# A planned attention and two-layer kernel: the planner's costs, the group sizes of two blocks, and the place of one block's sums

## The chip, the cores and the metric

The kernel runs on one core of a Trainium2 chip. The metric is the device time of one execution in microseconds (us). The engines are TensorE (PE, with its weight loads PEld), VectorE (DVE), ScalarE (ACT), GpSimd (POOL) and SyncE (SP, which here only issues transfers). Each engine works off its own queue of instructions in order and waits on semaphores for the others.

## The reference

Eight batches, eight heads, 576 positions, head width 64. First a masked, decaying attention without softmax, then a two-layer network over the 4608 tokens that it yields:

```
scores = (1/sqrt(D)) * q @ k.T
Dmat   = where(rel >= 0, gamma[h] ** rel, 0)      # rel = i - j
x      = (scores * Dmat) @ v                      # to (tokens, heads*64)
h      = x @ w_in                                 # 512 -> 2048
out    = (h * cos(h)) @ w_out                     # 2048 -> 512
```

Inputs and output are float32. The kernel multiplies in bfloat16 and adds up in float32.

## The kernel before, in words

**Attention.** The work is cut into units `(b, g)`: batch `b`, and `g` = 0, 1 for 256 positions each, 2 for the last 64. A unit's q, k and v come in by three loads of 512 KB on SP (`stgq`, `stgk`, `stgv`, line 471). k is cast (`natk`, line 462), q and v are scaled by the decay (`qnat`, `natv`, line 504), mostly on POOL; the first two units are marked fast and use DVE and ACT too. k and q are then transposed: for blocks 0 and 1 by PE (line 525) with a copy out of PSUM by ACT or DVE, from block 2 on by SP's transposing transfers (`kt`, `qt`, line 540). PE makes the scores (`bk<-qt,kt`), DVE multiplies them by the triangular mask (four operations of 512 columns to a unit, `pt`, line 611), and PE makes the outputs (`bk<-pt,natv`, with `qt` times the running state, all on line 571). The state `st` is built by PE from k and v and copied out by ACT (`sba`, `sbb`, `sbr`). Two copies on ACT (line 461) bring a unit's outputs to `xt`. Two units, those of two neighbouring batches, fill one block of 512 tokens: block 0 is (0,0) and (1,0), block 1 (0,1) and (1,1), block 2 (2,0) and (3,0), block 3 (2,1) and (3,1), and so on; block 8 is made of the eight short units.

**First layer** (`mlp1`, lines 762 to 773). For each of 16 slices `f` of the hidden width, PE runs four matmuls into one of six PSUM banks (`bk<-xt,win`), ACT makes the sine (`cb`, line 770; a shift of pi/2 makes it a cosine), and DVE multiplies the two into `gt` (line 773). `ses` says which units of the block a group covers: one of them (256 tokens, a half group) or both (512, a full group). The order of the slices is `FORDER`: 0 to 3, 8 to 11, 4 to 7, 12 to 15, four for each of the four slabs of `win`, which arrive in the order 0, 2, 1, 3. Before, blocks 0, 1 and 2 are made by half groups: block 0 by a loop of its own in `graph`, which takes all halves of the first unit and then all of the second; blocks 1 and 2 by `SPLIT = 2`. Blocks 3 to 8 are made by full groups.

**Second layer** (`wino2`, lines 810 to 891). Each block needs 7 products P1 to P7 instead of 8, as in Strassen's and Winograd's scheme: halves of `gt` and quarters of `wout` are added and subtracted first. DVE makes eight sums for a block (S1 to S4, each in two parts of 1024 columns, `s`, lines 828 and 834), and once, for all blocks, eight differences of the weights (`wsums`, `tw` and `wout`, line 807). Each product is two pieces of eight matmuls (line 867: `bk<-wout,gt` for P1 and P2, `bk<-tw,s` for P6 and P5, `bk<-wout,s` for P7 and P3, `bk<-tw,gt` for P4). ACT copies three results aside (`sn`), DVE adds (`os`, line 879), and SP stores the two halves of a block.

**Weights.** `win` and `wout` come in by four loads each, issued by POOL (lines 742 and 746) and cast on the way. Loads on SP and POOL are gated on each other by hand (`gate`): the third unit's loads on `win` 2, `wout` on q of unit (1,1), and unit (2,0)'s loads on `wout` 2.

**The order of the work** is not written out by hand. `graph` makes a list of tasks, each with an engine, an estimated length, what it reads and writes, the buffers that it takes, and a priority, a due time derived from `T0`, `T1` and `PERIOD`. `Graph.run` then plays all of this through once, on the host, while the kernel is built: it puts each engine's tasks in the order in which they would start by the estimates, and hands out the buffers. The estimates are plain numbers in the code: `dma` and `tail` are a transfer's time on the shared DMA engines and from its end to its landing, and `port=True` keeps a DVE task and a POOL task from being planned at the same time. What comes out is one fixed queue for each engine. The estimates have no other effect: on the chip each instruction starts when its queue and its semaphores let it. A PE task that takes more than two PSUM banks can claim them when it is due (`due` in `pick`), so that smaller tasks do not take them one by one. Where the plan shows PE idle early on, the emitter puts in matmuls on a tile of ones (`warm`, line 409).

Of the kernel before, what the change touches and what calls it, by code (L numbers as in the profile page):

```python
# [11 lines left out]
B, H, S, D = 8, 8, 576, 64  # L12
# [117 lines left out]
class Graph:  # L130
# [3 lines left out]
    AHEAD, FETCH = 2000, 6500  # L134

# [72 lines left out]
    def run(self, dma_rate):  # L208
        self.prios()
        free = {e: 0.0 for e in ("pe", "act", "dve", "pool", "sp")}  # L210
# [3 lines left out]
        est, order = {}, []  # L214
# [19 lines left out]
        def pick(e):  # L234
            cand = []
            for t in ready[e]:
# [3 lines left out]
                s = max(free[e], est[t], a)  # L240
# [9 lines left out]
            if e == "pe":  # L250
                due = [t for t in ready[e] if all(any(f is not None and f <= free[e] + 1500 for f in self.pools[b.pool])
                                                  for b in t.allocs if b.pool != "bk") and self.first(t) and sum(b.pool == "bk" for b in t.allocs) > 2 and est[t] <= free[e] + 1500]
# [70 lines left out]
class Kernel:  # L323
# [7 lines left out]
    SPLIT = 2  # L331
# [127 lines left out]
    def copy(self, eng, dur, dst, src, r, w, **kw):  # L459
        if eng == "act":  # L460
            return self.one(eng, dur, lambda e: e.activation(dst(), src(), AF.Copy), r=r, w=w, **kw)  # L461
        return self.one(eng, dur, lambda e: e.tensor_copy(dst(), src()), r=r, w=w, port=True, **kw)  # L462


    def load(self, which, u, rows, gate):

        stg = self.staged[which, u] = Buf("stg" + which)
        src = self.src["qkv".index(which)]
        for i, (p0, n, o, ny, b, r0) in enumerate(rows):
            at, w = (b * H * S + r0) * D, ny * D  # L470
            self.one("sp", 500, lambda e, p0=p0, n=n, o=o, w=w, at=at: e.dma_start(  # L471
                ap(self.at(stg), 1024, p0, n, o, [w, H], [1, w]), bass.AP(src, at, [[w, n], [S * D, H], [1, w]])),
                r=gate, w=[(stg, i)], sem=lambda i=i: f"{which}{stg.slot}_{i}", dma=1830 if ny == 2 else 600, tail=720)
        return stg

    def unit(self, u, fast=False, gate=()):
# [3 lines left out]
        for which, nat, dst in (("k", "natk", "kt"), ("q", "qnat", "qt"), ("v", "natv", None)):  # L480
# [4 lines left out]
            stg = self.load(which, u, rows, gate)  # L485
            rs = [(stg, i) for i in range(len(rows))]
            nb = t[nat] = Buf(nat)
            for y in range(2):
# [8 lines left out]
                if which == "k":  # L497
                    eng = ("act", "pool")[y] if fast else "pool"
                    self.copy(eng, {"act": 520, "dve": 610, "pool": 560}[eng], out, inp, rs, [(nb, y)])
                else:  # L500
# [3 lines left out]
                    self.one(eng, 610 if eng == "dve" else 1000, lambda e, out=out, inp=inp, tab=tab, col=col, hs=hs: e.tensor_tensor(  # L504
                        out(), inp(), ap(tab, 40, 0, 128, col, *hs, [0, D]), ALU.mult),
                        r=rs + [(key,)], w=[(nb, y)], port=True)
# [29 lines left out]
    def txb(self, u):  # L536
        parts = []
# [6 lines left out]
        self.G.add("sp", 2600, parts, dma=4300)  # L544
# [104 lines left out]
    def outputs(self, u, prio, late, join=None):  # L649
# [57 lines left out]
        def copies():  # L707
            for s in range(2):
# [6 lines left out]
                self.copy("act", 590, dst, src, [(ob[s],)], [(xt, half, s)])  # L715
# [24 lines left out]
    def load_w(self, which, s, gate, prio):  # L740
# [4 lines left out]
        else:  # L745
# [4 lines left out]
                 sem=f"{which}{s}", dma=2600, tail=1500, prio=prio)  # L750
# [59 lines left out]
    def wino2(self, j, base, span):  # L810

        gt = self.gt[j]
        S_ = {(i, q): Buf("s") for i in range(1, 5) for q in range(2)}

# [9 lines left out]
        for q in range(2):  # L824
            for i, x, y, r, op in (
# [3 lines left out]
                         r=r, w=[(S_[i, q],)], port=True, name=f"S{i}_{j}")  # L829
        for q in range(2):  # L830
            for i, x, y, r, op in (
# [3 lines left out]
                         r=r, w=[(S_[i, q],)], port=True, name=f"S{i}_{j}")  # L835
# [71 lines left out]
    def graph(self):  # L907
# [103 lines left out]
```

## Time and profile before

| | us |
|---|---|
| median of 3 runs (302.33 to 304.1) | 303.77 |
| the profiled execution | 302.27 |
| its span, first to last instruction | 300.6 |
| PE busy (x3785 matmuls) | 284.7 |
| VectorE busy | 224.1 |
| ScalarE busy | 169.2 |
| GpSimd busy | 104.2 |
| mean granted TensorE clock | 0.999 |

The profile is one execution. A row of a timeline is: start, length, engine, line, operation, what it writes and reads, shape, count; in brackets the idle time of the engine ahead of it and what ended that. A row of a group ends with busy time, mean ns of one, and idle time ahead of them with what ended it. Lengths of neighbouring instructions overlap a little, since the engines are pipelined, so the time from start to start is shorter than the length. "L867" is line 867 of the kernel before; the kernel after has four lines more.

### The profile page before, as it was taken

Reading aid. Unit: us, or ns where it says so; the run is one execution under the profiler, and the core shown is the slowest. Engines: PE = TensorE matmul, PEld = TensorE weight load, DVE = VectorE, ACT = ScalarE, POOL = GpSimd, SP = SyncE. Lnnn points to the kernel's source line nnn. Section 1 sums busy time; section 2 is a strip of 40 time slices with the busy share of each in tenths; the row PEclk is TensorE's granted clock in tenths of the full one; section 3 lists DMA queues with packets and bytes.
Section 4 is the critical chain, followed back from the end, with each engine's and each line's share of the span. In section 5 each row is a group of like instructions: output and inputs, shape, how many; then the busy total and the mean of one; then the engine's idle time right before and its main releaser. Section 6 shows DMA issues by size and latency. Waiting matters only on the chain.

```text
span 300.6 us, 9042 instructions
## 1 busy us (share of the span) xinstructions
PE 284.7 (95%) x3785; PEld 202.8 (67%) x3785; DVE 224.1 (75%) x390; ACT 169.2 (56%) x315; POOL 104.2 (35%) x125
## 2 busy tenths in 40 slices
PE   7789799999898999999999999999999999999994
PEld 2457577788687876667676767666766676666683
DVE  3667998999994889697959595968687857666721
ACT  5468785468556565645564556465554574545420
POOL 3821970885749204826263515071100000000000
PEclk9999999999999999999999999999999999999999
DMA  7999799999999279996999995782103000300115
GB/s 202 252 206 287 185 180 233 258 240 315 252 274 227 63 186 285 217 226 203 184 301 199 262 218 115 175 218 65 37 1 142 2 2 2 140 0 2 71 72 140
DMA packets 101640, 49.87 MB, mean 166 GB/s; under 512 B 43488, under 2 KB 97248, under 8 KB 101600
## 3 DMA queue, kind: packets, MB, share of 16 engines
q1 hardware_dynamic: 97376, 45.10, 62.8%
q0 software_dynamic: 4224, 4.19, 8.7%
q8 instruction: 30, 0.49, 0.7%
q14 instruction: 10, 0.08, 0.1%
HBM read 36.70 MB, written 9.44 MB: 154 GB/s over the span
## 4 chain that ended last, share of the span: by engine, by line
PE 75%; DMA 13%; POOL 5%; ACT 2%; DVE 2%; issue 1%; SPq 0%; DVEq 0%
PE bk L762 35%; PE bk L867 33%; DMA stgq<-in_q_dram 7%; PE bk L571 6%; DMA wout<-in_moe_w_out_dram 4%; DMA win<-in_moe_w_in_dram 3%; POOL natv L504 2%; PE st L571 1%; POOL qnat L504 1%; ACT xt L461 1%; DVE gt L773 1%; ACT cb L770 0%; POOL wout L746 0%; DVE s L828 0%; SPq L471 0%
## 5 line engine op out<-in xcount | busy, mean ns | idle before, releaser
L770 ACT ACTIVATE cb<-bk,cpi 128x256 bf16<-128x256 f32 (+1 forms) x192 | 108.1, 584 | 82.5 <-PE bk L762 79.2
L762 PE MATMUL bk<-xt,win 128*128 128x256 bf16 (+1 forms) x768 | 143.2, 326 | 2.7 <-issue 1.5
L773 DVE TENSOR_TENSOR gt<-bk,cb 128x256 bf16<-128x256 f32 (+1 forms) x192 | 103.0, 553 | 50.1 <-ACT cb L770 46.5
L762 PEld LDWEIGHTS bk<-xt,win 128*128 128x128 bf16 x768 | 71.9, 98 | 40.6 <-issue 2.7
L504 POOL TENSOR_TENSOR natv<-stgv,wv 128x512 bf16<-128x512 f32 x36 | 40.0, 1134 | 34.6 <-PE bk L571 20.4
L611 DVE TENSOR_TENSOR pt<-bk,tr 128x512 bf16<-128x512 f32 x68 | 42.6, 679 | 2.8 <-PE bk L571 2.8
L504 POOL TENSOR_TENSOR qnat<-stgq,wq 128x512 bf16<-128x512 f32 x32 | 35.1, 1119 | 18.5 <-DMA stgq<-in_q_dram 18.5
L462 POOL CAST natk<-stgk 128x512 bf16<-128x512 f32 x34 | 21.9, 670 | 53.4 <-DMA stgk<-in_k_dram 40.9
L867 PE MATMUL bk<-wout,gt 128*128 128x256 bf16 x288 | 36.7, 273 | 2.4 <-DVE gt L773 1.5
L867 PE MATMUL bk<-tw,s 128*128 128x256 bf16 x288 | 36.9, 273 | 1.0 <-ACT xt L461 1.0
L867 PE MATMUL bk<-wout,s 128*128 128x256 bf16 x288 | 36.4, 273 | 0.0
L867 PEld LDWEIGHTS bk<-tw,s 128*128 128x128 bf16 x288 | 27.8, 98 | 9.7 <-ACT xt L461 1.2
L867 PEld LDWEIGHTS bk<-wout,gt 128*128 128x128 bf16 x288 | 27.6, 98 | 9.4 <-issue 1.8
L867 PEld LDWEIGHTS bk<-wout,s 128*128 128x128 bf16 x288 | 27.8, 98 | 6.5
L461 ACT ACTIVATE sn<-bk 128x512 f32<-128x512 f32 x27 | 16.1, 597 | 17.2 <-PE bk L867 17.2
L879 DVE TENSOR_TENSOR os<-bk,sn 128x512 f32<-128x512 f32 x27 | 18.4, 681 | 9.2 <-PE bk L867 9.2
L461 ACT ACTIVATE xt<-bk 128x512 bf16<-128x512 f32 x36 | 23.7, 728 | 0.5 <-PE bk L571 0.5
L867 PE MATMUL bk<-tw,gt 128*128 128x256 bf16 x144 | 18.5, 273 | 0.0
L867 PEld LDWEIGHTS bk<-tw,gt 128*128 128x128 bf16 x144 | 14.1, 98 | 4.2
L834 DVE TENSOR_TENSOR s<-gt 128x1024 bf16<-128x1024 bf16 x18 | 15.4, 858 | 0.2
L828 DVE TENSOR_TENSOR s<-gt 128x1024 bf16<-128x1024 bf16 x18 | 15.1, 836 | 0.5
L834 DVE TENSOR_TENSOR s<-gt,s 128x1024 bf16<-128x1024 bf16 x18 | 14.7, 815 | 0.2
(56 smaller groups left out, 166.9 us busy)
## 6 DMA issues: line engine op xcount, KB each, us to landing
stgk<-in_k_dram SPq DMA_DIRECT2D x16, 512.0 KB, 6.5
stgq<-in_q_dram SPq DMA_DIRECT2D x16, 512.0 KB, 7.1
stgv<-in_v_dram SPq DMA_DIRECT2D x16, 512.0 KB, 6.7
out_dram<-os SPq DMA_DIRECT2D x16, 512.0 KB, 3.2
win<-in_moe_w_in_dram POOLq DMA_DIRECT2D x4, 512.0 KB, 9.1
wout<-in_moe_w_out_dram POOLq DMA_DIRECT2D x4, 512.0 KB, 10.3
stgk<-in_k_dram SPq DMA_DIRECT2D x8, 128.0 KB, 3.5
stgq<-in_q_dram SPq DMA_DIRECT2D x8, 128.0 KB, 3.3
```

What stands on the lines that cost most here:

```text
L461: return self.one(eng, dur, lambda e: e.activation(dst(), src(), AF.Copy), r=r, w=w, **kw)
L462: return self.one(eng, dur, lambda e: e.tensor_copy(dst(), src()), r=r, w=w, port=True, **kw)
L504: self.one(eng, 610 if eng == "dve" else 1000, lambda e, out=out, inp=inp, tab=tab, col=col, hs=hs: e.tensor_tensor(out(), inp(), ap(tab, ...
L571: return lambda e: e.matmul(out(), lhs(), rhs(), start=start, stop=True, skip_group_check=True)
L611: self.one("dve", 610, lambda e, r=r, b=b, pt=pt: e.tensor_tensor(ap(self.at(pt), 1024, 0, 128, 512 * r, [64 * ny * ny, 8 // ny // ny], [1 ...
L762: inst = e.matmul(ap(self.at(bk), 512, 0, 128, 0, [1, n]), ap(self.WIN, 4 * DFF, 0, 128, c * DFF + 128 * f, [1, 128]), ap(self.at(xt), 204 ...
L770: self.one("act", 70 + n, lambda e: e.activation(ap(self.at(cb), TB, 0, 128, 0, [1, n]), ap(self.at(bk), 512, 0, 128, 0, [1, n]), AF.Sin, ...
L773: self.one("dve", 75 + n / 0.96, lambda e: e.tensor_tensor(ap(self.at(gt), NF * TB, 0, 128, f * TB + 256 * h0, [1, n]), ap(self.at(bk), 51 ...
L828: self.one("dve", 610, lambda e, i=i, q=q, x=x, y=y, op=op: e.tensor_tensor(sv(i, q), x(), y(), op), r=r, w=[(S_[i, q],)], port=True, name ...
L834: self.one("dve", 610, lambda e, i=i, q=q, x=x, y=y, op=op: e.tensor_tensor(sv(i, q), x(), y(), op), r=r, w=[(S_[i, q],)], port=True, name ...
L867: inst = e.matmul(ap(self.at(bank), 512, 0, 128, 256 * tt, [1, 256]), l(f, tt), rr(f), start=(first and f == 0 and tt == 0), stop=True, sk ...
L879: self.one("dve", 610, lambda e: e.tensor_tensor(view(h, c), ap(self.at(bank), 512, 0, 128, 0, [256, 2], [1, 256]), ap(self.at(sn[name]), ...
```

## The change

Nothing that is computed changes. Seven things do:

1. The scheduler's estimates. Loads: 1840 for 1830, and a tail of 1800 instead of 720 for units that are not fast. `win` 2750 and `wout` 3000 for 2600, with a tail of 1900 for 1500. Transposing transfers 3000 for 4300. POOL's cast 580 for 560, its products 1030 for 1000.
2. `port` is set for a copy or a scaling only when it runs on POOL; before also when it runs on DVE. The sums on DVE keep it.
3. `SPLIT = 1`: block 2's first layer goes by full groups.
4. Block 0's first layer goes by slices, both units in turn, and by full groups in the second half of `FORDER` (slices 4 to 7 and 12 to 15).
5. `late`: the eight sums of block 0 also depend on the first slab of `wout`, which they do not read.
6. `SWIFT`: one of the two copies to `xt` moves from ACT to DVE for units (0,0), (1,0) and (0,1).
7. `DUE`: the scores of unit (0,1), which take two banks in each part, may claim them when due.

```
-    SPLIT = 2
+    SPLIT = 1
+    HALVES = (0, 2)
+    SWIFT = ((0, 0), (1, 0), (0, 1))
...
-        return self.one(eng, dur, lambda e: e.tensor_copy(dst(), src()), r=r, w=w, port=True, **kw)
+        return self.one(eng, dur, lambda e: e.tensor_copy(dst(), src()), r=r, w=w, port=eng == "pool", **kw)
...
-                r=gate, w=[(stg, i)], sem=lambda i=i: f"{which}{stg.slot}_{i}", dma=1830 if ny == 2 else 600, tail=720)
+                r=gate, w=[(stg, i)], sem=lambda i=i: f"{which}{stg.slot}_{i}", dma=1840 if ny == 2 else 600, tail=720 if fast else 1800)
...
-        self.G.add("sp", 2600, parts, dma=4300)
+        self.G.add("sp", 2600, parts, dma=3000)
...
-                self.copy("act", 590, dst, src, [(ob[s],)], [(xt, half, s)])
+                self.copy("dve" if s and u in self.SWIFT else "act", 590, dst, src, [(ob[s],)], [(xt, half, s)])
...
-                 sem=f"{which}{s}", dma=2600, tail=1500, prio=prio)
+                 sem=f"{which}{s}", dma=2750 if which == "win" else 3000, tail=1900, prio=prio)
...
+        late = [("wout", 0, 0)] * (j == 0)
...
-                         r=r, w=[(S_[i, q],)], port=True, name=f"S{i}_{j}")
+                         r=r + late, w=[(S_[i, q],)], port=True, name=f"S{i}_{j}")
...
-        for h in range(2):
-            for i, f in enumerate(self.FORDER):
-                self.mlp1(0, f, (h,), T0 + 435 * (2 * i + h))
+        for i, f in enumerate(self.FORDER):
+            for ses in ((0,), (1,)) if f // 4 in self.HALVES else ((0, 1),):
+                self.mlp1(0, f, ses, T0 + 435 * (2 * i + ses[0]))
```

The planned queues of the two kernels differ from the first microseconds on. PE's, around the change (m1 a half group, m2 a full one, T a transpose, SC scores and OUT outputs of a unit, P1 to P7 pieces of the second layer): before, "m1, 7 m1, OUT(1,0), 24 m1 with T, SC and OUT of (0,1) among them, then pieces of block 0's P1 and P6, m1 of block 1, SC and OUT (1,1) ...". After, "m1, OUT(1,0), 15 m1, 7 m2 with T among them, SC(0,1), 1 m2, OUT(0,1), 6 m1 of block 1, P1, SC(1,1) ... all of block 1's m1 and block 0's P, SC(2,0), P1 of block 1, OUT(2,0), P2, P6, part of P5, SC(3,0), P5, P7, OUT(3,0), P3, then block 2's m2". DVE's queue after has block 0's sums, the weight differences and the masks of (1,1) behind the first slab's landing, and all eight sums of block 1 in a row between the masks of (2,0) and those of (3,0). SP's queue after puts the transposes of (2,0) behind two more loads, and those of (3,0) behind the first store of an output.

More of the change, by code (lines that the diff above doesn't have):

```diff
@@ L484, in unit @@
                 rows = [(0, 128, 0, 2, u[0], 256 * u[1])]
-            stg = self.load(which, u, rows, gate)
+            stg = self.load(which, u, rows, gate, fast)
             rs = [(stg, i) for i in range(len(rows))]
@@ L498, in unit @@
                     eng = ("act", "pool")[y] if fast else "pool"
-                    self.copy(eng, {"act": 520, "dve": 610, "pool": 560}[eng], out, inp, rs, [(nb, y)])
+                    self.copy(eng, {"act": 520, "dve": 610, "pool": 580}[eng], out, inp, rs, [(nb, y)])
                 else:
```

11 lines of the change are left out of this document (6 added, 5 removed).

## The prediction

> **What bounds the kernel now.** I read the totals, then busy time by stage, then the tensor engine's (PE) timeline for its gaps, then the queues of VectorE (DVE), GpSimd (POOL) and SyncE (SP) up to each gap. First two lines of the page, and the stages (columns: window, length, busy time of PE, PEld, DVE, ACT, POOL with counts, granted clock, DMA share, GB/s):
>
> ```profile
> span 300.6 us, 9042 instructions
> PE 284.7 (95%) x3785; PEld 202.8 (67%) x3785; DVE 224.1 (75%) x390; ACT 169.2 (56%) x315; POOL 104.2 (35%) x125
> ```
> ```profile
> 0.00:17.00 17.00, 12.93 (x192) 6.63 (x192) 8.51 (x28) 8.81 (x15) 10.63 (x25) 1.00 0.99 224
> 17.00:23.50 6.50, 5.22 (x104) 4.16 (x104) 4.99 (x12) 3.89 (x9) 0.00 (x0) 1.00 1.24 207
> 23.50:41.20 17.70, 15.45 (x235) 11.88 (x232) 15.13 (x33) 14.32 (x34) 12.59 (x15) 1.00 0.96 222
> 41.20:74.80 33.60, 32.25 (x488) 26.80 (x484) 31.39 (x56) 21.56 (x48) 18.90 (x19) 1.00 1.14 254
> 74.80:84.70 9.90, 8.36 (x161) 6.60 (x161) 9.84 (x19) 5.20 (x12) 8.08 (x8) 1.00 1.19 255
> 84.70:120.00 35.30, 34.34 (x568) 27.07 (x566) 28.77 (x57) 21.31 (x47) 13.28 (x16) 1.00 0.82 203
> 120.00:284.00 164.00, 163.73 (x1940) 108.76 (x1939) 120.58 (x185) 91.08 (x148) 40.76 (x45) 1.00 0.55 126
> ```
>
> From 120 us on PE is busy 163.73 of 164 us: nothing that leaves PE's work as it is can win there. The gaps lie before, 1.28+2.25+1.35+1.54+0.96 = 7.4 us from 17 to 120, and two engines share the blame: DMA is full until 85 us, and DVE is at 31.39 of 33.6 and 9.84 of 9.9. So the change is worth what it takes from those 7.4 us, less what it adds.
>
> **Rates.** PE's rows in the chain of waits (start, length, work), DVE's and ACT's groups by shape:
>
> ```profile
> 62.71 2.22 PE bk L762 x20
> 259.00 1.73 PE bk L762 x8
> 60.09 0.87 PE bk L867 x8
> ```
> ```profile
> L773 DVE TENSOR_TENSOR gt<-bk,cb 128x512 bf16<-128x512 f32 x96 | 65.5, 688 | 39.2 <-ACT cb L770 38.0 <-PE bk L867 0.5
> L611 DVE TENSOR_TENSOR pt<-bk,tr 128x512 bf16<-128x512 f32 x68 | 42.6, 679 | 2.8 <-PE bk L571 2.8
> L773 DVE TENSOR_TENSOR gt<-bk,cb 128x256 bf16<-128x256 f32 x96 | 37.4, 419 | 10.9 <-ACT cb L770 8.5 <-PE bk L762 2.0
> L828 DVE TENSOR_TENSOR s<-gt 128x1024 bf16<-128x1024 bf16 x18 | 15.1, 836 | 0.5
> ```
> ```profile
> L770 ACT ACTIVATE cb<-bk,cpi 128x512 bf16<-128x512 f32 x96 | 66.1, 689 | 64.2 <-PE bk L762 63.8
> L770 ACT ACTIVATE cb<-bk,cpi 128x256 bf16<-128x256 f32 x96 | 42.0, 480 | 18.3 <-PE bk L762 15.4 <-DVE gt L773 2.8
> ```
>
> **Change, part 1: 512 tokens at once.** 24 pairs of half groups become full ones (16 in block 2, 8 in block 0). On PE two halves take 8 x 0.111 = 0.89 us and a full group 4 x 0.216 = 0.87: nothing. On DVE each pair saves 2 x 0.419 - 0.688 = 0.15 us, 3.6 in all, on ACT 0.27, 6.5 in all. Only DVE's share before 85 us can count, 8 x 0.15 = 1.2. The price is cover: half groups of block 2 could run after unit (2,0) alone, full ones need (3,0) too.
>
> **Part 2: 17 to 23.5 us.** PE's timeline, then DVE's:
>
> ```profile
> 16.99 0.61 PE L762 MATMUL bk<-xt,win 128*128 128x256 bf16 x4 [0.17 <-DMA win<-in_moe_w_in_dram]
> 17.53 0.44 PE L571 MATMUL st<-natv,natk 64*64 64x64 bf16 x16
> 20.44 2.12 PE L762 MATMUL bk<-xt,win 128*128 128x256 bf16 x18 [1.28 <-issue]
> 22.50 0.64 PE L571 MATMUL bk<-pt,natv 64*64 64x128 bf16 x32
> 40.12 0.64 PE L571 MATMUL bk<-pt,natv 64*64 64x128 bf16 x32
> 45.70 1.05 PE L867 MATMUL bk<-wout,gt 128*128 128x256 bf16 x8 [0.83 <-DMA wout<-in_moe_w_out_dram]
> 59.11 0.44 PE L571 MATMUL st<-natv,natk 64*64 64x64 bf16 x16 [0.52 <-POOL natv L504]
> 76.40 1.03 PE L867 MATMUL bk<-wout,gt 128*128 128x256 bf16 x8 [1.54 <-DVE gt L773]
> 82.77 0.64 PE L571 MATMUL bk<-pt,natv 64*64 64x128 bf16 x32
> 94.43 1.05 PE L867 MATMUL bk<-tw,s 128*128 128x256 bf16 x8 [0.96 <-ACT xt L461]
> ```
> ```profile
> 16.40 2.48 DVE L611 TENSOR_TENSOR pt<-bk,tr 128x512 bf16<-128x512 f32 x4 [0.80 <-PE bk L571]
> 30.85 1.52 DVE L828 TENSOR_TENSOR s<-gt 128x1024 bf16<-128x1024 bf16 x1
> 32.30 1.53 DVE L834 TENSOR_TENSOR s<-gt 128x1024 bf16<-128x1024 bf16 x1
> 36.29 0.68 DVE L828 TENSOR_TENSOR s<-s,gt 128x1024 bf16<-128x1024 bf16 x1
> ```
>
> GpSimd's timeline there, and the time from issue to landing of the second layer's weights:
>
> ```profile
> 31.79 2.94 POOL L504 TENSOR_TENSOR natv<-stgv,wv 128x512 bf16<-128x512 f32 x2
> 35.23 3.04 POOL L746 DMA_DIRECT2D wout<-in_moe_w_out_dram  x4
> 38.25 2.09 POOL L504 TENSOR_TENSOR qnat<-stgq,wq 128x512 bf16<-128x512 f32 x2
> ```
> ```profile
> DMA to landing us min/median/max: 5.9/10.3/12.9
> ```
>
> Before, PE ran four half groups, waited 1.28 us for the second slab of weights, and did unit (1,0)'s outputs at 22.5. Now one half group comes first, then those outputs, then 15 halves. The outputs wait for the four masks, done at 18.88 before and some 0.4 us sooner now (DVE no longer puts q products between the masks of (0,0), and takes one copy of x off ACT): one half group 16.95 to 17.4, a gap of about 1.1, outputs to 19.6, seven halves at 0.44 to 22.6, where before the same work (with (1,0)'s state products, the 0.44 at 17.53, which now run while the slab is still on its way) ended at 23.5. Gain 0.9; ends 0 (the masks gain nothing and the copy delays the next x) and 2.0 (no gap). The four q products that DVE does at the start are no longer kept apart from GpSimd's; only one of them falls beside a v product, at most 1.05 us (half of the 2.09 for two) and, as the slab comes last here, I count nothing. GpSimd's fourth weight load moves behind two products, but the loads before it still queue, so it lands as before.
>
> **Part 3: 23.5 to 41.2, the held sums.** Three sums ran on DVE here, 1.52+1.53+0.68 = 3.7 us, ahead of unit (0,1)'s masks. They go. Left on PE from 22.6: 8 halves (3.5), 7 full groups (6.1), transposes (0.9): 33.1. Then a chain: ACT's copy of q to 33.6, scores to 34.4, one full product on DVE to 35.1, four masks at 0.62 to 37.6. Outputs of (0,1) start at 37.75 instead of 40.12: 2.4 us ahead, part 2 included. Ends: 0.9, and 3.7.
>
> The second weights: one more k cast now stands ahead of the weight loads, but the v products lose their collision with the sums (2.94 against 2.09 for two), so the issue stays at 35.1 and slabs land from 41.1 (35.23+5.9) to 50.4 (37.5+12.9). The new wait on the first slab therefore costs nothing: the first sum's turn on DVE comes near 47, behind ten products, the first weight difference and four masks.
>
> **Part 4: 38.8 to 74.8 on PE.** New gap: with no second-layer work allowed before the slab, PE waits 1.1 us for (0,1)'s x, then runs six half groups of block 1 (2.6) and reaches the second layer near 43. Later gaps about 0.8. Against that 0.83, 0.52 and 1.54 disappear. On PE alone the lead is 2.4 - 1.9 + 2.9 = 3.4 us, and 0.2 for four transposes done earlier: 3.6 when (2,0) is through. Ends: 2.5 if the later gaps are twice that, 4.7 if (0,1)'s x costs no gap.
>
> **Part 5: the bill on DVE, 37.6 to 84.** Moved past the slab, all eight sums of block 0, eight weight differences, and all eight sums of block 1 (the order puts these, in a row, ahead of (3,0)'s masks) stand in DVE's queue before (3,0)'s outputs: 24 operations of 1024 columns, where before 18 stood there. The rest up to there: 32 half products at 0.385 start to start (12.3), 12 masks and 4 additions at 0.61 (9.7, as four masks took 2.48), one full product and one copy of x at the same rate (1.2): 23.2. Idle: 2.6 until the six groups deliver, 0.5 later. So the masks end at 37.6 + 23.2 + 3.1 + 24u. The unknown is u. Low end 0.62 (0.68 less overlap, the row at 36.29), high end 1.45 (1.52, GpSimd busy). I take 0.84: by the queues GpSimd pauses twice (for block 2's loads and for (3,0)'s transposes), so about half of the 24 run at 0.62 and the other half I put midway, 1.04; the group's mean of 0.836 is nearest. The masks then end at 84.1; PE alone would want them at 82.2.
>
> How that compares: after (3,0)'s outputs (1.4 us) and two more pieces of second layer (1.75), so at 87.2, PE has twelve pieces of block 1's second layer behind it, 12 x 0.87 = 10.4. Before, at 84.7, it had three of them and eight half groups of block 2, 2.6 + 3.5 = 6.1. The 4.3 us between make 84.7 worth 89.0: lead 1.8.
>
> The Trainium skill, page "SBUF — State Buffer", section "Who interferes with whom", says that a VectorE operation with two SBUF inputs and a GpSimd operation that reads SBUF lock each other out for the whole instruction. The row at 30.85 beside GpSimd's products agrees (1.52 against 0.68). By it alone, with every sum behind a whole GpSimd product, u would be 0.62 + 1.05 = 1.67 and the masks would end at 104; the row gives 0.83 more, not 1.05, and only where GpSimd is at work, so I keep 0.84.
>
> **Part 6: other moves.** SP's queue, a load's issue and the transposes' landing times up to 100 us:
>
> ```profile
> 48.84 1.75 SPq L471 DMA_DIRECT2D stgv<-in_v_dram  x1
> ```
> ```profile
> DMA to landing us min/median/max: 5.7/6.5/7.8
> ```
>
> Transposes of (2,0) now follow two more loads on SP, 2 x 1.75 later; the order has (2,0)'s scores near 67 us, as much later, so PE covers it with block 1's groups. Those of (3,0) follow an output store that waits for block 0's last addition near 68: issue at 68.5, landing by 76.4 at the longest row, against a need at 78.7. Hidden by 2.3 us, dearer one for one after that. The copies of x on DVE, the scheduler's new times and the rule that lets (0,1)'s scores claim two free banks only set the order, and are in the parts above. From block 3's first layer on the order is nearly the old one. The 0.96 gap (row at 94.43) belonged to block 1's second layer, done by then; for new gaps in block 2 I set 0.4, between 0 and the 0.96 that they replace: 0.6 gained.
>
> **Sum.** 1.8 + 0.6 = 2.4 us off the profiled span: 298.2. The profiled execution took 302.27 us (span plus 1.67), now 299.9; the median of runs is 303.77, 1.5 above it, so 301.4 there.
>
> **Rivals.** *Full lead:* DVE's sums fall into GpSimd's pauses, u at or under 0.76; the masks then end when PE wants them, lead 3.6 + 0.6: 299.6 by the median. For it: sums in GpSimd's pause took 0.68. Against: DVE was at 31.39 of 33.6 already.
> *Gaps only move:* u near 0.94 gives masks at 86.5, lead -0.6, +0.6: 303.8. For it: a full DVE queue just passes the time on.
> *Slower:* the lock keeps hitting the eight sums of block 1, which stand in a row before (3,0)'s masks with no block 2 half groups left as cover. Above u = 0.94 it is slower than before; at 1.1 the masks end at 90.3, lead -4.4+0.6: 307.6. For it: 1.52 and 1.53 twice in a row above; against: a third of the stretch has no GpSimd work.
> *Cold clock:* these rows are the first warm-up matmuls and later ones:
>
> ```profile
> 1.12 4.02 PE L409 MATMUL bk<-one 128*128 128x512 bf16 x9 [1.12 <-DVE lg L432]
> 8.49 1.03 PE L409 MATMUL bk<-one 128*128 128x512 bf16 x4
> ```
>
> 0.45 us each at first, 0.26 later; the change runs 24 in place of 25. Were the clock lost after a gap, 4 us at half speed would cost 2: 303.4. But 1.54 us of gap at 76.4 lost nothing. The Trainium skill ("TensorE: Matmul & The Clock Gate", "What's actually happening") lets the clock fall after about 3.4 us of idling; no gap that I expect is so long.
>
> **Chances.** Forecast (1 to 4 us gained) 0.48, full lead 0.19, gaps only move 0.18, slower 0.13, cold clock 0.02. 1% is 3.0 us, about what a measurement can tell from no change: faster 0.36 (the full lead and the best third of the forecast), same 0.50, slower 0.14 (the cold clock counted with it). Range 298.0 to 305.4: from 1.6 us beyond the full lead (part 4's upper end) to u near 1.01. The forecast's own: 299.8 to 302.8.
>
> **What would show it.** Right: outputs of (0,1) near 37.8, no wait over 0.5 us for win, second layer from 43, masks of (3,0) ending near 84, sums averaging 0.9 there, PE full from 90. Wrong: outputs of (3,0) after 87 (u), a wait on its transposes (SP), or gaps beyond 90.

## The result and the profile after

| | before | after |
|---|---|---|
| median (20 runs each) | 303.84 | 301.08 |
| lowest to highest | 300.53 to 306.25 | 299.54 to 306.34 |
| the profiled execution, its span | 302.27, 300.6 | 301.32, 299.6 |
| mean granted clock in it | 0.999 | 0.992 |

After stands to before as 0.9924, 95% interval [0.99, 0.9947], or 2.3 us less; disturbed executions, over 1.5% above the fastest of the same kernel, are left out of this ratio and of those below. The forecast was 301.4 us, 2.4 less. The gain is under the 1% that the prediction took as about the least to be told from no change, but the interval does not reach 1.

The two profiles show only 1.0 us of it. First the totals of the kernel after and its stages, cut where those of before were cut (window, length, busy time of PE, PEld, DVE, ACT, POOL with counts, granted clock, DMA share, GB/s):

```profile
span 299.6 us, 8757 instructions
PE 284.8 (95%) x3688; PEld 194.9 (65%) x3688; DVE 222.4 (74%) x369; ACT 164.3 (55%) x288; POOL 107.2 (36%) x125
```
```profile
17.00:23.50 6.50, 5.61 (x85) 4.47 (x85) 3.22 (x7) 3.41 (x8) 0.00 (x0) 0.74 1.24 207
23.50:41.20 17.70, 16.08 (x213) 10.15 (x211) 13.67 (x25) 14.44 (x28) 12.59 (x16) 1.00 1.00 227
41.20:74.80 33.60, 32.72 (x425) 27.36 (x423) 31.03 (x60) 19.42 (x43) 20.47 (x19) 1.00 1.12 241
74.80:84.70 9.90, 9.43 (x199) 7.92 (x200) 9.90 (x14) 3.64 (x7) 6.14 (x6) 1.00 1.10 260
84.70:120.00 35.30, 34.15 (x550) 20.22 (x539) 29.17 (x44) 22.77 (x40) 19.75 (x22) 1.00 1.11 250
120.00:284.00 164.00, 163.31 (x1938) 108.54 (x1936) 121.35 (x187) 89.78 (x146) 37.64 (x40) 1.00 0.48 120
```

PE's idle time from 17 to 120 us is 0.89 + 1.62 + 0.88 + 0.47 + 1.15 = 5.0 us, against 7.4 before. But the second window has a clock of 0.74 where before had 1.00, so its 5.61 busy microseconds hold less work, and from 120 on PE is busy for 163.31 us in place of 163.73. PE's timeline, for the steps that the prediction named:

```profile
17.94 0.78 PE L765 MATMUL bk<-xt,win 128*128 128x256 bf16 x4 [0.89 <-DMA win<-in_moe_w_in_dram]
18.65 1.07 PE L574 MATMUL bk<-pt,natv 64*64 64x128 bf16 x32
...
38.94 0.64 PE L574 MATMUL bk<-pt,natv 64*64 64x128 bf16 x32
...
41.05 1.05 PE L765 MATMUL bk<-xt,win 128*128 128x256 bf16 x8 [0.45 <-ACT xt L464]
...
44.13 1.04 PE L871 MATMUL bk<-wout,gt 128*128 128x256 bf16 x8
...
84.33 0.64 PE L574 MATMUL bk<-pt,natv 64*64 64x128 bf16 x32 [0.47 <-DVE pt L614]
...
87.14 3.62 PE L765 MATMUL bk<-xt,win 128*128 128x512 bf16 x16
...
110.96 0.42 PE L574 MATMUL bk<-qt,kt 64*64 64x128 bf16 x16 [0.97 <-DVE gt L776]
```

The 0.89 us ahead of 17.94 are a wait for the first slab of `win`, which landed 6.6 us after its issue; before, it took 5.6. The outputs of (1,0) start at 18.65 (forecast 18.5), those of (0,1) at 38.94 (forecast 37.75; before 40.12), the second layer at 44.13 (forecast 43), the outputs of (3,0) at 84.33 after 0.47 us of waiting for their masks, and block 2's first full group at 87.14 (forecast 87.2). The last row is a new gap. DVE around the same places:

```profile
36.31 2.47 DVE L614 TENSOR_TENSOR pt<-bk,tr 128x512 bf16<-128x512 f32 x4
...
50.74 0.69 DVE L832 TENSOR_TENSOR s<-s,gt 128x1024 bf16<-128x1024 bf16 x1
...
57.22 1.53 DVE L810 TENSOR_TENSOR wout<-wout 128x1024 bf16<-128x1024 bf16 x1
...
75.91 1.70 DVE L832 TENSOR_TENSOR s<-s,gt 128x1024 bf16<-128x1024 bf16 x2
...
79.74 2.13 DVE L838 TENSOR_TENSOR s<-gt,s 128x1024 bf16<-128x1024 bf16 x2
81.80 2.47 DVE L614 TENSOR_TENSOR pt<-bk,tr 128x512 bf16<-128x512 f32 x4
84.20 0.67 DVE L883 TENSOR_TENSOR os<-bk,sn 128x512 f32<-128x512 f32 x1
```

The four masks of (0,1) take 2.47 us and start at 36.31. The sums of block 0 and the weight differences now run between 45 and 80 us: 0.69 us each while GpSimd has nothing to do (50.74), 1.53 beside its v products from 56.71 on (57.22). Two rows of block 1's sums, two in each, stand ahead of the masks of (3,0), which end when the next instruction starts, at 84.20. GpSimd:

```profile
31.54 2.04 POOL L507 TENSOR_TENSOR natv<-stgv,wv 128x512 bf16<-128x512 f32 x2
...
34.94 3.04 POOL L749 DMA_DIRECT2D wout<-in_moe_w_out_dram  x4 [0.25 <-DMA stgq<-in_q_dram]
```

The two v products took 2.94 us beside the sums and now take 2.04; the issue of the second weights stays at 34.94.

Last, the granted clock (the third figure from the end of a row) in four windows; the first shows how little PE did ahead of the fall:

```profile
14.00:18.00 4.00, 2.21 (x55) 1.03 (x53) 3.08 (x6) 1.16 (x3) 2.79 (x3) 1.00 1.21 199
...
18.20:18.60 0.40, 0.40 (x4) 0.07 (x1) 0.00 (x0) 0.00 (x0) 0.00 (x0) 0.56 1.24 207
...
20.00:21.00 1.00, 1.00 (x22) 0.69 (x19) 0.53 (x1) 0.59 (x2) 0.00 (x0) 0.50 1.25 209
...
21.40:21.80 0.40, 0.40 (x4) 0.33 (x3) 0.00 (x0) 0.40 (x2) 0.00 (x0) 0.67 1.24 202
```

If the clock has two values, 0.56 and 0.67 put the fall at 18.25 us and its end at 21.66: 3.4 us at half speed. The profile before has 1.00 throughout that stretch. The longest idle time in PE's timeline from 14 us up to there is the 0.89 us ahead of 17.94.

### The profile page after: what moved, and what is told of

It is laid out like the page before. It is cut to its first block, busy times and chain, and to the rows that moved or that the text cites. A ratio compares the mean times of both kernels' runs of the same rounds, so it can differ in the third digit from the quotient of the medians.

```text
span 299.6 us, 8757 instructions
## 1 busy us (share of the span) xinstructions
PE 284.8 (95%) x3688; PEld 194.9 (65%) x3688; DVE 222.4 (74%) x369; ACT 164.3 (55%) x288; POOL 107.2 (36%) x125
## 3 DMA queue, kind: packets, MB, share of 16 engines
q1 hardware_dynamic: 97376, 45.10, 61.9%
## 4 chain that ended last, share of the span: by engine, by line
PE 80%; DVE 8%; DMA 4%; ACT 3%; issue 2%; POOL 1%; SPq 0%; DVEq 0%; POOLq 0%
PE bk L765 39%; PE bk L871 33%; PE bk L574 7%; DVE gt L776 3%; DMA stgv<-in_v_dram 2%; DMA win<-in_moe_w_in_dram 2%; ACT cb L773 2%; DVE pt L614 2%; PE st L574 1%; DVE s L832 1%; DVE s L838 1%; POOL natv L507 1%; ACT qt L464 1%; DVE wout L810 0%; SPq L474 0%
## 5 line engine op out<-in xcount | busy, mean ns | idle before, releaser
L773 ACT ACTIVATE cb<-bk,cpi 128x512 bf16<-128x512 f32 (+1 forms) x168 | 103.8, 628 | 87.4 <-PE bk L765 87.0
L765 PE MATMUL bk<-xt,win 128*128 128x512 bf16 (+1 forms) x672 | 142.9, 350 | 3.0 <-DMA win<-in_moe_w_in_dram 0.9
L776 DVE TENSOR_TENSOR gt<-bk,cb 128x512 bf16<-128x512 f32 (+1 forms) x168 | 100.4, 611 | 50.0 <-ACT cb L773 49.2
L765 PEld LDWEIGHTS bk<-xt,win 128*128 128x128 bf16 x672 | 63.8, 98 | 47.0 <-issue 2.3
L507 POOL TENSOR_TENSOR qnat<-stgq,wq 128x512 bf16<-128x512 f32 x32 | 36.8, 1169 | 26.9 <-DMA qt<-qnat 13.7
L465 POOL CAST natk<-stgk 128x512 bf16<-128x512 f32 x34 | 23.6, 718 | 40.5 <-PE bk L574 14.5
L464 ACT ACTIVATE sn<-bk 128x512 f32<-128x512 f32 x27 | 16.1, 597 | 17.8 <-PE bk L871 17.8
L464 ACT ACTIVATE xt<-bk 128x512 bf16<-128x512 f32 x33 | 21.7, 723 | 0.5 <-PE bk L574 0.5
L871 PE MATMUL bk<-tw,gt 128*128 128x256 bf16 x144 | 18.5, 273 | 0.0
L838 DVE TENSOR_TENSOR s<-gt,s 128x1024 bf16<-128x1024 bf16 x18 | 15.4, 858 | 0.2
L574 PEld LDWEIGHTS bk<-qt,kt 64*64 64x64 bf16 x576 | 8.8, 106 | 8.7 <-issue 2.7
L838 DVE TENSOR_TENSOR s<-gt 128x1024 bf16<-128x1024 bf16 x18 | 14.3, 793 | 0.2
```

The costliest lines, as they stand in the source:

```text
L507: self.one(eng, 610 if eng == "dve" else 1030, lambda e, out=out, inp=inp, tab=tab, col=col, hs=hs: e.tensor_tensor(out(), inp(), ap(tab, ...
L574: return lambda e: e.matmul(out(), lhs(), rhs(), start=start, stop=True, skip_group_check=True)
L765: inst = e.matmul(ap(self.at(bk), 512, 0, 128, 0, [1, n]), ap(self.WIN, 4 * DFF, 0, 128, c * DFF + 128 * f, [1, 128]), ap(self.at(xt), 204 ...
L773: self.one("act", 70 + n, lambda e: e.activation(ap(self.at(cb), TB, 0, 128, 0, [1, n]), ap(self.at(bk), 512, 0, 128, 0, [1, n]), AF.Sin, ...
L776: self.one("dve", 75 + n / 0.96, lambda e: e.tensor_tensor(ap(self.at(gt), NF * TB, 0, 128, f * TB + 256 * h0, [1, n]), ap(self.at(bk), 51 ...
L838: self.one("dve", 610, lambda e, i=i, q=q, x=x, y=y, op=op: e.tensor_tensor(sv(i, q), x(), y(), op), r=r + late, w=[(S_[i, q],)], port=Tru ...
```

## The experiments

My theory after the result: the changed order gains what the prediction says, and the clock takes part of it back in some executions; the hold is needed by this order. The rivals: the gap between the profiles is the whole effect; the hold does nothing, since DVE has the same work either way; the new transfer times or the full groups carry the gain. Three parts of the change were never taken out by themselves beside the hold: `port`, `SWIFT` and `DUE`. No kernel leaves out work. Each is the changed kernel with the edit shown, if nothing else is said; times of the kernel before in the same sets of runs were 303.03, 303.08, 303.48 and 303.12 us (medians).

### The clock

**More fillers.** The emitter puts matmuls on a tile of ones into PE's early gaps; here twice as many, other than in the first run of them.

```
-                    self.warm(max(1, self.G.fill(gap, warm)))
+                    self.warm(max(1, (2 if warm else 1) * self.G.fill(gap, warm)))
```

> The changed kernel with twice the warm-up matmuls in each planned gap but the first; the queues are otherwise the same. If the half clock seen from 18.2 to 21.7 us in the changed kernel's profile comes from too little PE work before the first weights land: granted clock 1.00 from 17 to 23 us, eight half groups done 1 to 1.7 us earlier, most runs at a mean clock of 0.998 or more, and a ratio to the kernel before of 0.985 to 0.990. If the half clock is chance: clocks spread as before (some runs near 0.993) and a ratio of 0.991 to 0.996; longer fillers in the way could also cost up to 0.5 us.

Measured: 300.36 us, ratio 0.9914 [0.9887, 0.9941]. Its windows and its PE timeline:

```profile
14.00:18.00 4.00, 3.79 (x67) 2.04 (x64) 3.23 (x7) 1.62 (x5) 2.77 (x3) 1.00 1.23 204
...
17.00:22.70 5.70, 5.13 (x90) 4.11 (x88) 3.93 (x9) 3.42 (x9) 0.00 (x0) 1.00 1.25 207
```
```profile
18.40 0.95 PE L574 MATMUL bk<-pt,natv 64*64 64x128 bf16 x32 [0.50 <-DVE pt L614]
...
37.71 0.64 PE L574 MATMUL bk<-pt,natv 64*64 64x128 bf16 x32
...
42.92 1.04 PE L871 MATMUL bk<-wout,gt 128*128 128x256 bf16 x8
...
83.62 0.64 PE L574 MATMUL bk<-pt,natv 64*64 64x128 bf16 x32
```

PE is now busy for 3.79 of the 4 us up to 18, the clock stays at 1.00, and the outputs of (0,1) come at 37.71, the second layer at 42.92 and the outputs of (3,0) at 83.62. These are the forecast's 37.75 and 43 to 0.1 us. Here the first slab landed early, too, so a second run tells the clock from the slab: the version with block 2 by halves (below) has the order of the kernel after up to there, the same fillers and the same late slab, starts the outputs of (1,0) at 18.58 and kept its clock:

```profile
37.59 0.64 PE L574 MATMUL bk<-pt,natv 64*64 64x128 bf16 x32
```

So the 1.2 us by which the first profile missed the forecast here was the clock. Of the 1.2 us at 38, 0.7 is left at 84, where DVE sets the time, and what is left of it at the end is not clear: the ratio, 0.9914, lies within the interval of the kernel after and in the range that was expected if the fall is chance. All six executions kept the clock, but of the kernel after 12 of 17 did, at which rate six in a row come about one time in eight.

**Fillers in the first stretch only.**

```
-                if gap > 400 and self.wb.left:
+                if gap > 400 and self.wb.left and not warm:
```

> The changed kernel with only the first nine warm-up matmuls. If filler work holds the clock: half clock in most of the stretch from 10 to 24 us, mean clock 0.96 to 0.985, 2 to 5 us slower than the changed kernel (ratio to before 0.998 to 1.01). If the clock does not hang on the fillers: clocks as in the changed kernel and a ratio of 0.991 to 0.995.

Measured: 306.3 us, ratio 1.011 [1.0072, 1.0148]. One window:

```profile
17.00:22.70 5.70, 4.83 (x84) 3.58 (x81) 3.27 (x7) 2.35 (x5) 0.00 (x0) 0.50 1.23 204
```

The clock is at half in all of it, and the outputs of (0,1) start at 40.74. Five of the six executions have a mean clock of 0.971 to 0.977, so the later fillers hold the clock in most of them, and without them the whole gain is lost and more. The clock need not be all of the loss: the sixth had 0.994 and was the slowest, 307.82 us.

**Old transfer times** (with GpSimd's casts and products at 560 and 1000 again), and then old times with the fillers doubled.

```
-  dma=1840 if ny == 2 else 600, tail=720 if fast else 1800
+  dma=1830 if ny == 2 else 600, tail=720
-  dma=2750 if which == "win" else 3000, tail=1900        (slabs)
+  dma=2600, tail=1500
-  dma=3000                                                (transposes)
+  dma=4300
```

> The changed kernel with the scheduler's old transfer times (loads, transposes, weight slabs, copies), everything else as changed. Theory, the times only set an order and the hold carries the gain: 300.8 to 303.0 us, ratio 0.992 to 0.999, outputs of (0,1) still before 40.12 us. Rival, the times carry the gain, because with the old ones units are called for before their transposes have landed: ratio 0.999 to 1.006, and gaps of over 1 us on the tensor engine that end with a transpose or a load.

> The changed kernel with the old transfer times (by itself 300.32 us with a granted clock of 0.992 to 0.994 in all four executions) and with twice the later fillers. Clock theory: the stretch from 14 to 18 us had the tensor engine busy for 2.14 of 4 us and lost the clock each time; filled, it is kept: clock 0.997 or more in nearly all executions, and 0.5 to 1.2 us less: 299.1 to 299.9 us, ratio 0.987 to 0.990. Rival, the clock falls for another reason, or what it costs is covered by VectorE's queue: 300.0 to 300.6 us.

Measured: 300.32 us, ratio 0.9918 [0.989, 0.9946], and with the fillers 299.62, ratio 0.9872 [0.9836, 0.9909]. The new times are not what the change lives on: with the old ones it is as fast, though PE waits again for `wout` (0.90 us, at 45.40). The first of the two lost the clock in each of its four executions (0.992 to 0.994), and its stretch is the emptiest:

```profile
14.00:18.00 4.00, 2.14 (x56) 1.15 (x55) 3.21 (x6) 1.30 (x3) 2.80 (x3) 1.00 1.19 195
```

With the fillers two of six still had 0.994, and the median is 0.7 us lower; the intervals of the two just overlap. This is the fastest version of the study, ahead of both kernels; how it stands to the changed kernel itself was not measured side by side.

**Control: the kernel before with its fillers doubled.**

> The kernel before, with twice the filler matmuls after the first run of them (the edit that took the changed kernel to 300.36 us). Clock theory: the granted clock of the kernel before is 1.00 in every microsecond from 10 to 24 us, so more fillers have nothing to mend: ratio to the kernel before 0.998 to 1.003. Rival, fillers shorten any version of this kernel, by whatever they do to the order or the buffers: ratio 0.996 or less, and then the gain seen with them says nothing about the clock.

Measured: 303.54 us, executions from 300.55 to 311.99, ratio 0.9973 [0.9941, 1.0004] by the six below 304 us. This does not tell the two apart. It also corrects what I had taken from one profile. A mean clock under 0.9955 is what one fall gives (3.4 us at half speed are 1.7 of 300). Among the 63 executions of the kernel before that the ratios of these runs use, 12 had it, too (median 304.67 us, the other 51 303.02). Of the 17 of the kernel after that its ratio uses, 5 had it (301.32, the other 12 300.76). So a fall goes with 1.6 us before; after, with 0.6, from five executions that reach from 300.14 to 302.84.

### The hold

**Without it**, and then also without the copies of x on DVE.

```
-        late = [("wout", 0, 0)] * (j == 0)
+        late = []
...
-    SWIFT = ((0, 0), (1, 0), (0, 1))
+    SWIFT = ()                              (the second kernel only)
```

> The changed kernel without the hold on block 0's sums (all else as changed; the planner replans). Mine: the sums stand ahead of (0,1)'s masks again, so the outputs of (0,1) start 1.5 to 3.5 us later than in the changed kernel's profile (38.94), and the gain against the kernel before shrinks to a ratio of 0.996 to 1.002 in place of 0.9924. Rival (the new order of block 0 does it, the hold is idle): outputs of (0,1) within 0.5 us of 38.94 and a ratio of 0.990 to 0.995.

> The changed kernel without the hold (305.48 us by itself) and with all copies to x back on ScalarE. There the tensor engine waited 1.91 us at 43.6 us for a copy to x that stood on VectorE behind two sums. If that copy in VectorE's queue is what the missing hold costs: the 1.91 us gap is gone and the time is 303.0 to 304.3 us. If the sums themselves are the cost (masks, half products and weight differences behind them), whoever makes the copy: 304.8 to 306.5 us.

Measured: 305.48 us, ratio 1.0067 [1.0034, 1.0099], and 304.22, ratio 1.0048 [1.0009, 1.0087]. The first is slower than either expectation allowed, and not where mine had put it: the outputs of (0,1) start at 39.79, only 0.85 us after the changed kernel's (both profiles lost the clock at 18 us). The loss comes behind that. Two rows of the first one's PE timeline, and DVE's queue ahead of the first:

```profile
43.58 1.03 PE L765 MATMUL bk<-xt,win 128*128 128x256 bf16 x8 [1.91 <-DVE xt L465]
...
61.90 0.61 PE L765 MATMUL bk<-xt,win 128*128 128x256 bf16 x4 [1.58 <-DVE os L883]
```
```profile
40.16 1.19 DVE L838 TENSOR_TENSOR s<-gt,s 128x1024 bf16<-128x1024 bf16 x1
41.27 1.53 DVE L832 TENSOR_TENSOR s<-gt 128x1024 bf16<-128x1024 bf16 x1
42.72 0.71 DVE L465 CAST xt<-bk 128x512 bf16<-128x512 f32 x1
```

Two sums of 1.19 and 1.53 us stand ahead of the copy that brings x to PE's next work; the same happens with an addition at 61.9. With the copy on ACT that gap is gone, and the time lies in the range that was expected if the copy was the cause. But PE's timeline has another gap of the same size a microsecond later, and DVE one very long sum ahead of it:

```profile
44.77 0.38 PE L528 MATMUL bk<-idn,natk 128*128 128x128 bf16 x4 [1.90 <-issue]
```
```profile
38.38 3.78 DVE L838 TENSOR_TENSOR s<-gt,s 128x1024 bf16<-128x1024 bf16 x1
```

This sum ran while GpSimd was at work (from 37.97 to 43.05 without a pause). Two more follow it, and ScalarE waits 2.04 us for the half product behind them, at 44.25. So the copy is not shown to be the cause by itself; the intervals of the two versions overlap. In both profiles it is what stands behind two or three early sums on DVE that comes late: the copy in one, and, as I read the second, half products in the other. That PE's 1.90 us hang on the half product is argued from ScalarE's wait; the profile names no releaser for PE.

**The hold alone**, put into the kernel before.

> The kernel before with the hold alone: block 0's eight sums read the first slab of the second weights too, and nothing else is changed. If the hold is what the change lives on (without it the changed kernel ran at 1.0067), it does most of the work alone: 300.8 to 302.3 us, ratio 0.991 to 0.997, outputs of (0,1) two to three us before 40.12. Rival, hold and new order need each other, because the old order keeps half groups of unit (0,1) and the early claim of two banks out: ratio 0.998 to 1.005, outputs of (0,1) after 39.

Measured: 307.49 us, ratio 1.0119 [1.006, 1.0177], with the outputs of (0,1) at 39.34: the rival, and worse than it allowed. Its DVE and PE:

```profile
53.46 1.09 DVE L807 TENSOR_TENSOR wout<-wout 128x1024 bf16<-128x1024 bf16 x1
54.47 1.53 DVE L835 TENSOR_TENSOR s<-gt 128x1024 bf16<-128x1024 bf16 x1
55.93 1.53 DVE L807 TENSOR_TENSOR wout<-wout 128x1024 bf16<-128x1024 bf16 x1
57.38 2.97 DVE L835 TENSOR_TENSOR s<-gt,s 128x1024 bf16<-128x1024 bf16 x2
```
```profile
60.84 1.68 PE L762 MATMUL bk<-xt,win 128*128 128x256 bf16 x8 [3.00 <-DVE gt L773]
```

The held sums and the weight differences come free together, and in the old order five of them stand in a row on DVE in these rows, 1.1 to 1.5 us each. The half products behind them are late, and PE waits for 3.00 us, until one of them is done. In the changed order four stand in a row from 50.14 to 52.55, too, but at 0.69 us each, since GpSimd starts only at 52.45; beside GpSimd's products, no more than two of them are in a row without a half product (as at 56.55 and 57.22, or 62.52 and 63.80). So the hold costs 1.2% in the old order and is worth 3 to 4 us (305.48 to 301.08; 303.89 to 300.76 over executions that kept the clock) in the new one. Its value cannot be told apart from the order that the planner makes with it.

**Held twice.** With the doubled fillers, block 1's eight sums wait too, until the last mask of (3,0) is written.

```
-  late = [("wout", 0, 0)] * (j == 0)
+  late = [("wout", 0, 0)] * (j == 0) + ([(self.tiles[3, 0]["pt", 1], 1)] if j == 1 else [])
```

> The changed kernel with twice the later fillers (300.36 us by itself), and with block 1's eight sums also held, until the masks of unit (3,0) are written. Theory, VectorE has the same work to do and only its order changes: the masks of (3,0) end near 80 in place of 83.5, the tensor engine then waits for the sums in block 1's second layer, and the time stays within 0.7 us of 300.36 (299.7 to 301.0). Rival, the eight sums in a row ahead of those masks are a bill that a better order does not pay (part 5 put it at 1.9 us, 84.1 against 82.2): 298.5 to 299.3 us.

Measured: 304.7 us, ratio 1.005 [1.0018, 1.0082]: both expectations failed, by 3.7 us and more. Its PE, DVE and one window:

```profile
77.67 0.64 PE L574 MATMUL bk<-qt,kt 64*64 64x128 bf16 x32
80.92 1.07 PE L574 MATMUL bk<-pt,natv 64*64 64x128 bf16 x32 [2.60 <-DVE pt L614]
```
```profile
77.78 0.69 DVE L883 TENSOR_TENSOR os<-bk,sn 128x512 f32<-128x512 f32 x1 [3.20 <-PE bk L871]
78.39 2.47 DVE L614 TENSOR_TENSOR pt<-bk,tr 128x512 bf16<-128x512 f32 x4
80.90 2.72 DVE L832 TENSOR_TENSOR s<-gt 128x1024 bf16<-128x1024 bf16 x2
```
```profile
81.00:85.00 4.00, 4.00 (x99) 3.12 (x100) 4.00 (x5) 1.85 (x4) 2.07 (x2) 0.63 0.95 256
```

The masks end 2.4 to 3.3 us earlier (the next instruction starts at 80.90; with the doubled fillers alone they end at 83.3, in the kernel after at 84.2). They need the scores, whose transposes land at 76.2 here and which PE runs at 77.67, behind two pieces of second layer. DVE stands idle for 3.20 us ahead of an addition and the masks, PE has no sums to work with and waits for 2.60, and then the mean clock of four microseconds is 0.63. The eight sums in a row, which part 5 counted as a bill, filled time in which DVE had nothing else to do.

### The group sizes

**Block 2 by halves again** (`SPLIT = 2`), and **block 0 in its old order by halves**, alone and with the doubled fillers.

```
-        for i, f in enumerate(self.FORDER):
-            for ses in ((0,), (1,)) if f // 4 in self.HALVES else ((0, 1),):
-                self.mlp1(0, f, ses, T0 + 435 * (2 * i + ses[0]))
+        for h in range(2):
+            for i, f in enumerate(self.FORDER):
+                self.mlp1(0, f, (h,), T0 + 435 * (2 * i + h))
```

> The changed kernel with block 2 by half groups again; the two queues are the same up to the first pieces of block 1's second layer. Mine: neutral, since DVE pays 2.5 us more for halves and PE gains cover while it waits for (3,0): ratio 0.990 to 0.996, outputs of (3,0) not before 84, the eight sums of block 1 spread out. Rival (the full groups are what made the gain, by freeing DVE): ratio 0.997 to 1.003, DVE busy over 95 percent from 74 to 100 us and PE waiting for products there.

> The changed kernel with block 0's first layer in its old order: 16 half groups of unit (0,0), then 16 of (1,0), no full groups. Theory: what comes early is lost again in VectorE's queue by 84 us, so it is worth little: 301.0 to 302.5 us, ratio 0.993 to 0.998; outputs of (1,0) near 22 us, and those of (0,1) near 38.5 (eight pairs more of half products on VectorE, 1.2 us). Rival, the new order of block 0 is what the change lives on: ratio 0.999 or above, outputs of (0,1) near 40.

> The changed kernel with block 0's first layer in its old order by halves (301.82 us by itself) and with twice the later fillers. Clock theory: there the same stretch was busy for 3.07 of 4 us already and the clock fell in two of six executions, so the fillers bring 0.3 to 1 us: 300.8 to 301.5 us. Rival, fillers do nothing here: 301.6 to 302.2 us. For part 1: if it stays 0.5 us or more behind the 300.36 us of the changed kernel with the same fillers, full groups in block 0 are worth that; if not, they are worth nothing.

Measured: 301.23 us, ratio 0.9946 [0.9921, 0.9972], for block 2; 301.82, ratio 0.9956 [0.9913, 0.9998], for block 0, and with the fillers 301.08, ratio 0.9923 [0.988, 0.9965]. Block 2's group size makes no difference that these runs can tell from none. Block 0's is worth perhaps 0.7 us (301.08 against 300.36), within the intervals. The outputs of (1,0) stay early without the new order (18.40; I had expected 22). With the fillers the outputs of (0,1) even start earlier, at 37.11 (37.71 with the fillers alone), but the lead is given back far behind the change:

```profile
140.16 1.89 PE L765 MATMUL bk<-xt,win 128*128 128x512 bf16 x8 [1.74 <-DVE gt L776]
```

Block 2's run has one more use. Up to 18 us its order is that of the kernel after, and so are its times to 0.1 us, yet its clock stayed:

```profile
14.00:18.00 4.00, 2.23 (x56) 1.03 (x53) 3.15 (x6) 1.23 (x3) 2.80 (x3) 1.00 1.22 201
...
20.00:21.00 1.00, 1.00 (x12) 0.90 (x10) 0.47 (x1) 1.00 (x4) 0.00 (x0) 1.00 1.24 208
```

## Why the prediction was right

**Size.** 2.4 us were forecast. Taken over executions that kept the clock, before has 303.02 and after 300.76: 2.3 us. The profiled pair shows 1.0 for two reasons: the profiled execution of before was 0.75 us under that median, and that of after, which had lost the clock, 0.56 over its own. That the size came out to 0.1 us is luck in part: two terms of the sum, the lead at 87 us with the clock kept and what follows behind it, were off in opposite directions (below).

**Part 2** (gain 0.9) held as an order; its start, 18.65 for 18.5, came out by another way. It had the half group at 16.95 and a wait of 1.1 behind it, for the masks. In the profile the masks were written by 17.8, and PE waited ahead of the half group, for a slab that landed 1 us later than in the profile before; the sign "no wait over 0.5 us for win" failed. With the doubled fillers the slab landed early, and the sequence is the forecast's: half group at 17.31, then a wait for the masks, of 0.50. In the first profile half clock then took nearly all of the 0.9. With the clock kept, (0,1)'s outputs are where parts 2 and 3 had put them.

**Part 3** (lead 2.4 at (0,1)): 1.2 in the profile after, 2.4 with the fillers (40.12 to 37.71), 2.5 with block 2 by halves (37.59). The masks, the v products and the unmoved issue were right to 0.2 us.

**Part 4**: no wait on `wout` before the second layer, and 0.45 us for x behind 0.6 of fillers, for 1.1. Right, and late by the same 1.2 (44.13; 42.92 with the fillers, for 43).

**Part 5**: the masks of (3,0) ended at 84.20 for 84.1, with its unknown right and errors beside it that cancel. The 24 operations take 19.5 us from start to start in DVE's timeline, 0.81 each for the 0.84 that was taken (0.89 in length, for 0.9): twelve of them at 0.60 to 0.67, twelve at 1.02 on average, as the part had split them. They began 1.2 us late, as the four masks of (0,1) ended at 38.78; idle time was 3.55 (0.65, 1.43, 0.43, 0.43 and 0.61) for 3.1; and what is left for the other work is 22.4 for 23.2. The Trainium skill ("SBUF — State Buffer", "Who interferes with whom") has a two-input VectorE operation and GpSimd's reads lock each other out; the rows at 50.74 and 57.22 agree in direction, 0.69 against 1.53 us. What the step had wrong is the alternative: it put the price of the sums at 1.9 us against PE, which "alone would want them at 82.2". In the run with the second hold the masks ended at 80.90, and that run is 4 us slower: masks ahead of the sums are not a gain by themselves.

**Part 6**: right. Scores of (3,0) at 80.49 met no wait for a transpose.

**After 87 us** the forecast was 0.6 gained; 0.6 was lost by PE's idle time, and 0.9 by the spans (a lead of 1.9 at 87.14, by the prediction's way of comparing, and 1.0 at the end). The 0.96 gap went, but new ones came (1.15 us idle up to 120, 0.97 of it for a product on DVE, at 110.96), and 0.42 more idle time after 120, where the order was "nearly the old one". With the doubled fillers it is the same: block 2 starts at 86.43, a lead of 2.6, and the span is 298.8, 1.8 less than before. That is the term that failed, by about 1.4 us; it was set without a row for it, and "gaps beyond 90" was one of the prediction's own signs of being wrong. The lead of 2.6 in place of 1.8 where the clock is kept hid most of it in the total. Why PE meets the new gaps was not tested.

**Cold clock.** It was given 0.02, on the ground that a gap of 1.54 us had lost nothing and that no gap would be near 3.4. Both were true, and the clock fell all the same. The argument looked at the longest gap and not at how busy PE is over a stretch, which goes with the falls better: 2.21 of the 4 us up to 18, where before had

```profile
14.00:18.00 4.00, 3.77 (x109) 2.43 (x99) 2.51 (x6) 2.01 (x5) 2.54 (x3) 1.00 1.24 204
```

Its price of 2 us was near what it costs on the spot (3.4 us at half speed are 1.7, of which 1.2 showed at (0,1)'s outputs), but executions of the kernel after that lose the clock end only 0.6 us later (1.6 before). Its chance was far off: 5 of 17.

**Gaps only move** and **slower** did not come, but they were near: the hold without the order, the order without the hold, and a second hold all ended slower than before.

## What to carry to other kernels

When a change moves work between engines through a planner, its parts do not add up: try each part alone and the whole without it before giving any of them a price. Ahead of a prediction, read PE's busy share over stretches of some 4 us, and not its longest gap only; here 13 more fillers, four of them in the emptiest stretch, kept the clock in six executions of six, with a median 0.7 us lower than in the set of the kernel after (0.3 by the ratios, whose intervals overlap). Sums that stand ahead of a late operation may be filling its wait: see when its inputs come before counting them as a delay.

## What the runs showed of the hardware

The granted clock fell to 0.50 for 3.4 us, in the kernel after without a gap of over 0.89 us ahead of it. Worked out as above, the falls run from 18.25 to 21.66 in the kernel after and from 18.58 to 21.99 without the hold, from 61.06 to 64.47 with the hold alone (behind the gap of 3.00 us) and from 80.54 to 83.96 with the second hold (behind the gap of 2.60): 3.41 or 3.42 us each time. The same order of instructions kept it in one execution and lost it in another, with PE's times equal to 0.1 us up to that point, so it hangs on something that the program does not set.

How often the mean clock is under 0.9955 goes, roughly, with how busy PE was from 14 to 18 us in the profiled execution: 2.14 us, four executions of four; 2.21, 5 of 17; 2.23, 4 of 10; 2.29 (no hold), 5 of 9; 2.51 (no hold, copies on ACT), 3 of 9; 2.58 (old times with fillers), 2 of 6; 3.07 and 3.41 (block 0 by halves, and with fillers), 2 of 6 and 1 of 8; 3.79, none of six. The mean does not say where the clock fell, and the hold alone (3.63; 3 of 4) and the second hold (3.09; 8 of 10) have their own falls later. The kernel before does not fit into this row (3.77, and 12 of 63), but it has a wait of 1.28 us and sparse work behind 18 us. Nor is the busy time the program's alone: the run with the second hold has the same work up to 18 us as the one with the doubled fillers, and 3.09 for 3.79, mostly because its first slab landed 0.9 us later.

The Trainium skill ("TensorE: Matmul & The Clock Gate", "What's actually happening") has a window of about 3.4 us that runs freely, whatever the kernel does: the length of the fall and its chance from run to run agree. That the clock falls after an idle window does not: in the 3.41 us ahead of the fall at 18.25 PE was busy for 1.91. What share of work is enough, these runs leave open; and why single gaps of 2.60 and 3.00 us were followed by half clock, where 1.54 us at 76.4 before, and 1.91 and 1.90 without the hold, lost nothing.

A sum of 128x1024 takes 0.69 us on DVE while GpSimd is idle, mostly up to 1.53 beside its products, and 3.78 once (38.38, without the hold and the copies on DVE).
